# One product group of the first superstep split in two, under a newly drawn order of all instructions (linear attention and gated MLP, one core)

## The chip, the cores and the metric

The kernel runs on one core of a Trainium2 chip. The metric is the device time of one execution in microseconds; the engines are named PE (TensorE, matrix products), DVE (VectorE), ACT (ScalarE), POOL (GpSimd) and SP (SyncE, which here issues all DMAs).

## The reference

Two stages. The first is a recurrence over 768 positions for 4 x 8 heads of width 40, the second a gated MLP over the 3072 tokens that come out of it:

```python
for t in range(S):
    y[:, :, t] = einsum('bhd,bhde->bhe', rt, state)
    Sa = einsum('bhde,bhe->bhd', state, at)
    state = state * wt[:, :, None, :] - einsum('bhd,bhe->bhde', Sa, bt) + einsum('bhd,bhe->bhde', vt, kt)
...
h = x @ w_in                                     # 3072x320 @ 320x2048
g = h * erf(softplus(h))
out = g @ w_out                                  # 2048x320
```

All arrays are float32 values; the MLP's weights arrive in a wider type and are rounded to float32 on the chip.

## The kernel before

**Stages.** The 768 positions are cut into 6 stretches of 128 for each of 2 groups of 16 heads: 12 *supersteps* (0 to 11), each of 4 *chunks* of 32 positions. Superstep 0 delivers the first 256 rows of x; superstep q's MLP part can start when its four chunks are done. The state is carried from chunk to chunk (tile MT), so the chunks are a chain. The MLP is not: it is 96 blocks of 512 values per partition (8 to a superstep) that only need x.

**Names.** Below, "op q.c" is the operation of chunk c in superstep q; letters a to d tell the copies of one chunk apart.
- Once a superstep: w (load), wchk, scanS and scanP (L439, L443, two scans each), rG: the running products of the decays.
- A, ahead of the chain, per chunk: kba (load), ab and bk (DVE L472, L477), A (PE L482), Am a/b (DVE L489), bT and bTc (PE L500 and a copy), zs (DMA, waits for ab), AD (DMA of the masked products to DRAM).
- T, per superstep, for all four chunks at once: Ti and Ap (DMAs back from DRAM, after the last AD), 14 pairs Tm/Ts (DVE L529, L530: a triangular inverse), TD and tb (DMAs out and back), R (DVE L538), W, Wm, DAD (PE L547 and a copy), Tb (DVE L554).
- Chain, per chunk: zmm a/b (two copies of MT), Z (PE L593), zt (copy), U (PE L602), us (copy), zu a to d (four copies into tile Vu, L612), and beside these pmt and ysM (PE L618 and a copy of the old state), UT (PE L627), vtu (copy), PQ (PE L636), PQm (DVE L639, into Vu), then **MY** (PE L647 and L651), MT (DVE L654, state += MY's first 40 columns), Ym (DVE L658, the rows of y from the other 32 columns). MTs scales the state between supersteps.
- Out and in: xw (DMA of y to DRAM), xr (DMA back as x), xh and xl (x rounded and the rest), mm1 (PE L823), hc, tanh, ln, ln2, exp, nd, rho, gelu, E, G (ACT and DVE), mm2 (PE L878).
- Weights, once, at the start: wd (loads of 512 KB; "wd" of w_in, "wdo" of w_out), w1, w3, w5 (DVE L737 to L739), whi, whr, wr0 (ACT), wd_ (PE L754, L755), wlo (copies).
- warm (PE L422): 190 products whose result nobody reads, all ahead of the third mm1.

**MY.** For each of 4 pairs j, four products `sg x Vu` of 72 columns write the bank `my`: columns 0 to 39 are the state's update and need zu and the v rows of Vu, columns 40 to 71 are the rows of y and need PQm. Four products `sm x rt` of 32 columns are then added to columns 40 to 71.

**Order.** Nothing is scheduled on the chip: `Plan.schedule` returns the list ORDER, a permutation of the 4630 operations, and ENGINES, one letter for each (which of its allowed engines runs it). Each engine works through its own operations strictly in the list's order and waits at the head of its queue; data dependences (and reuse of buffers) are the waits. So an operation late in the list holds back what stands behind it on its engine, also DMAs on SP.

Of the kernel before, what the change touches and what calls it, by code (L numbers as in the profile page):

```python
# [1008 lines left out]
```

## Time and profile before

| | |
|---|---|
| runs shown | 756.65, 761.78, 762.60 us; median 761.78 |
| profiled execution | span 754.8 us, first to last instruction; its own device time is not listed apart from these runs |
| PE | 722.7 us busy (96%), 190 warm products included |
| DVE, ACT, POOL | 643.1 (85%), 573.3 (76%), 5.6 (1%) |
| DMA | 94.63 MB, all issued by SP |
| mean granted TensorE clock | 0.991 of full speed |

The profile is one execution. Its 40 slices of 18.9 us show PE at 9 tenths or more from slice 11 on, and at 6 to 9 before. PE's busy share of the opening says little by itself, as most of what runs there until about 110 us are weight preparation and warm products. The timeline of an engine tells what stood at the head of its queue, and in brackets how long it idled before and for whom.

### The profile page before, as it was taken

The page shows a single profiled execution, that of the slowest core. Times are in us where ns is not written, and L with a number is a line of the kernel's source. Part 1 is how long each engine was busy: PE and PEld are TensorE (multiplying, and loading weights), DVE is VectorE, ACT ScalarE, POOL GpSimd, SP SyncE. Part 2 cuts the span into 40 slices and gives each one's busy share as a digit, 9 for nine tenths or more (in the row PEclk, how much of TensorE's full clock was granted, in tenths as well). Part 3 has the DMA queues.
Part 4 walks back from the last instruction along what each step waited for, and adds up shares of the span by engine and source line. Part 5 has one row for each costly group of instructions (what it writes and reads, how often), then busy time and mean ns, then how long its engine had stood idle before and what let it go on. Part 6 is the DMA issues. An engine that isn't in the chain of part 4 may idle for free.

```text
span 754.8 us, 32087 instructions
## 1 busy us (share of the span) xinstructions
PE 722.7 (96%) x13807; PEld 570.4 (76%) x13807; DVE 643.1 (85%) x1461; ACT 573.3 (76%) x1122; POOL 5.6 (1%) x15
## 2 busy tenths in 40 slices
...
GB/s 255 175 256 197 142 160 153 144 124 122 129 147 121 131 140 126 118 125 126 131 126 136 132 134 139 130 104 138 140 103 115 124 112 92 104 41 61 21 17 22
DMA packets 165616, 94.63 MB, mean 125 GB/s; under 512 B 115452, under 2 KB 148988, under 8 KB 165468
## 3 DMA queue, kind: packets, MB, share of 16 engines
...
q8 instruction: 110, 1.80, 1.1%
...
HBM read 73.48 MB, written 14.16 MB: 116 GB/s over the span
## 4 chain that ended last, share of the span: by engine, by line
PE 83%; ACT 5%; DVE 5%; DMA 3%; issue 2%; SPq 1%; DVEq 0%
PE po L878 29%; PE ph L823 22%; PE my L647 4%; PE ph L422 4%; PE pA L547 4%; PE pQ L636 4%; PE pA L482 3%; PE my L602 2%; PE my L593 2%; PE pA L500 2%; PE pQ L618 2%; PE my L651 2%; SPq L381 1%; PE pQ L627 1%; ACT l L831 1%
## 5 line engine op out<-in xcount | busy, mean ns | idle before, releaser
L878 PE MATMUL po<-wo,h 128*128 128x320 f32 x768 | 265.2, 454 | 1.1 <-DVE h L869 1.1
L878 PEld LDWEIGHTS po<-wo,h 128*128 128x128 f32 x768 | 125.5, 189 | 30.5 <-DVE h L869 1.9
L831 ACT ACTIVATE l<-l 128x512 f32<-128x512 f32 x192 | 111.0, 624 | 8.3 <-DVE nd L856 7.5
L823 PE MATMUL ph<-xh,wih 128*128 128x256 f32 x384 | 113.8, 378 | 0.0
L823 PEld LDWEIGHTS ph<-xh,wih 128*128 128x128 f32 x384 | 69.5, 190 | 24.1 <-issue 0.3
L823 PE MATMUL ph<-xh,wil 128*128 128x256 f32 x384 | 77.2, 282 | 0.7 <-issue 0.7
L823 PE MATMUL ph<-xl,wih 128*128 128x256 f32 x384 | 76.9, 282 | 0.0
L856 DVE TENSOR_TENSOR nd<-l,r 128x512 f32<-128x512 f32 x96 | 64.3, 687 | 9.6 <-ACT r L831 8.4
L868 DVE TENSOR_TENSOR l<-l,r 128x512 f32<-128x512 f32 x96 | 64.5, 682 | 1.2 <-ACT l L831 0.4
L869 DVE SCALAR_TENSOR_TENSOR h<-l,h 128x512 f32<-128x512 f32 x96 | 64.6, 684 | 0.5
L857 DVE SCALAR_TENSOR_TENSOR r<-nd,r 128x512 f32<-128x512 f32 x96 | 64.2, 683 | 0.2
L831 ACT ACTIVATE l<-h 128x512 f32<-128x512 f32 x96 | 57.6, 627 | 4.2 <-DVE h L377 3.1
L823 PEld LDWEIGHTS ph<-xh,wil 128*128 128x128 f32 x384 | 59.5, 190 | 0.7 <-issue 0.7
L375 ACT COPY h<-ph 128x512 f32<-128x512 f32 x84 | 48.9, 583 | 14.2 <-PE ph L823 13.4
L823 PEld LDWEIGHTS ph<-xl,wih 128*128 128x128 f32 x384 | 59.2, 189 | 0.0
L831 ACT ACTIVATE r<-r 128x512 f32<-128x512 f32 x96 | 55.3, 623 | 0.4
L831 ACT ACTIVATE r<-l 128x512 f32<-128x512 f32 x96 | 54.9, 621 | 0.3
L422 PE MATMUL ph<-d 104*128 104x512 bf16 x190 | 53.3, 401 | 1.6 <-DVE d L392 1.6
L823 PE MATMUL ph<-xl,wir 128*128 128x256 f32 x192 | 54.2, 282 | 0.0
L823 PE MATMUL ph<-xh,wir 128*128 128x256 f32 x192 | 54.1, 282 | 0.0
L375 ACT COPY Zm<-MT 40x320 f32<-40x320 f32 x62 | 28.3, 457 | 28.7 <-DVE MT L654 24.1
L489 DVE TENSOR_TENSOR Zs<-pA,tri 64x256 f32<-64x256 f32 x96 | 40.6, 423 | 11.1 <-PE pA L482 6.0
...
## 6 DMA issues: line engine op xcount, KB each, us to landing
...
```

The lines of the kernel that those rows point to most:

```text
L375: self.nc.scalar.copy(o, i)
L422: P.add("warm", "PE", lambda e: nc.tensor.matmul(s.ph[1], s.d1[:, :128], s.d1[:, :512], start=True, stop=True), ["d1"], ["phw"], -1e3, 0.22)
L489: P.add("Am", "DVE", lambda e, x=x, xs=xs: nc.vector.tensor_tensor(out=zx[64:128, x], in0=pz[xs], in1=s.tri[xs, None, :].to_broadcast([64, ...
L547: nc.tensor.matmul(pw[js, i, ts], l[js, i], r[js, i, ts], start=True, stop=True)
L636: nc.tensor.matmul(pq[i % 2 * 64:i % 2 * 64 + 64, i // 4, i // 2 % 2], vr[:, 256 + n_ * 64:320 + n_ * 64], vr.rearrange("p (a x) -> p a x" ...
L823: nc.tensor.matmul(ph[:, j * 256:j * 256 + 256], a[:k, fs], b[:k], start=(m == 0), stop=(m == 7))
L831: self.P.add(name, "ACT", lambda e: nc.scalar.activation(out=o, in_=i, **kw), rd, wr + ["act"], pr, 0.62)
L856: P.add("nd", [("DVE", 0.69)], lambda e, r=r, l=l, nd=nd: s.eng(e).tensor_tensor(out=nd, in0=l, in1=r, op=ALU.mult), [("l", il), ("r", ir) ...
L857: P.add("rho", "DVE", lambda e, r=r, nd=nd: nc.vector.scalar_tensor_tensor(out=r, in0=nd, scalar=2 * C4, in1=r, op0=ALU.add, op1=ALU.mult) ...
L868: P.add("E", [("DVE", 0.69)], lambda e: s.eng(e).tensor_tensor(out=l, in0=l, in1=r, op=ALU.mult), [("r", ir)], [("l", il)], pr)
L869: P.add("G", "DVE", lambda e: nc.vector.scalar_tensor_tensor(out=h, in0=l, scalar=-1.0, in1=h, op0=ALU.add, op1=ALU.mult), [("l", il)], [( ...
L878: nc.tensor.matmul(po, h[:, bs], s.wo[:, f], start=(f == 0), stop=(f == 15))
```

## The change

Two things. (1) In superstep 0 alone (`NSPLIT = 1`, q < 1), MY is issued as two operations: MYs, the `sg x Vu` products on columns 0 to 39, which no longer waits for PQm, sm and rt; and MYy, the same products on columns 40 to 71 and the `sm x rt` products. MT waits for MYs alone, Ym for MYy alone. From superstep 1 on MY is one operation as before.

```diff
+NSPLIT = 1
...
-            ms("zmy", s.my[:, x], 0.0, ["my", "pz"], (("DVE", 0.6),))
+            ms("zmy", s.my[:, x], 0.0, ["my", "myr", "pz"], (("DVE", 0.6),))
...
+        py = my[:, :, :, 40:72].rearrange("p x j t -> p j x t")
+        split = q < NSPLIT
+
+        def mmy(e, state, rows):
+            fs = slice(0 if state else 40, 72 if rows else 40)
             for j in range(NP // 2):
                 for h in range(2):
                     for x in range(2):
                         xs = slice(x * 64, x * 64 + 64)
-                        nc.tensor.matmul(my[h * 64:h * 64 + 40, x, j], sg[xs, j, h], vu[xs, j // 2 * 2 + h, j % 2], start=True, stop=False)
-                for h in range(2):
+                        nc.tensor.matmul(my[h * 64:h * 64 + 40, x, j, fs], sg[xs, j, h], vu[xs, j // 2 * 2 + h, j % 2, fs], start=True, stop=not rows)
+                for h in range(2 * rows):
...
+        if split:
+            P.add("MYs", "PE", lambda e: mmy(e, True, False), [("sg", ig)] + kst, ["my"], pr, 0.6)
+            P.add("MT", "DVE", fmt, ["my"], ["MT"], pr, 0.49)
+            P.add("MYy", "PE", lambda e: mmy(e, False, True), [("sg", ig)] + krow, ["myr"], pr, 0.8)
+        else:
+            P.add("MY", "PE", lambda e: mmy(e, True, True), [("sg", ig)] + kst + krow, ["my", "myr"], pr, 0.95)
+            P.add("MT", "DVE", fmt, ["my"], ["MT"], pr, 0.49)
...
-        P.add("Ym", ..., ["my"], [("p", ip, c)], pro, 0.42)
+        P.add("Ym", ..., ["myr"], [("p", ip, c)], pro, 0.42)
```

(2) ORDER and ENGINES are other lists altogether (4634 operations). The DMAs' places in SP's queue, loads of input blocks and weights included, differ too. 271 operations run on another engine, most of them copies (108 of the 192 zu, 31 of the 96 zmm). The stretches of both lists that the prediction speaks of, with the numbers replaced by names ("warm*3" are three in a row):

```
PE, old list: 86 warm ahead of A 0.0
PE, new list: 56 warm ahead of A 0.0, with wd_ 0[0] and pmt 0.0 among them;
  A 0.0 | warm*4 | wd_ 0[1] | warm*6 | bT 0.0 | warm*2 | wd_ 0[2] | warm*13 | A 0.1

PE, old list, superstep 0's chain (74 warm):
U 0.0 | warm*2 | UT 0.0 | warm*3 | PQ 0.0 | A 1.1 | warm*1 | MY 0.0 | bT 1.1 | pmt 0.1 | warm*1 | Z 0.1 | warm*2 |
U 0.1 | warm*1 | A 1.2 | warm*1 | UT 0.1 | warm*3 | bT 1.2 | warm*1 | PQ 0.1 | warm*3 | A 1.3 | warm*1 | MY 0.1 |
bT 1.3 | warm*4 | pmt 0.2 | warm*1 | Z 0.2 | warm*1 | U 0.2 | UT 0.2 | warm*5 | PQ 0.2 | warm*6 | MY 0.2 | warm*1 |
wd_ 0[19] | warm*2 | wd_ 0[18] | pmt 0.3 | warm*1 | Z 0.3 | warm*1 | U 0.3 | warm*3 | UT 0.3 | warm*4 | PQ 0.3 |
warm*3 | MY 0.3 | warm*10 | Z 1.0 | ... | A 2.0 | warm*1 | U 1.0 | bT 2.0 | UT 1.0 | mm1 0[0]
PE, new list (71 warm):
U 0.0 | warm*3 | UT 0.0 | warm*1 | MYs 0.0 | warm*2 | A 1.1 | warm*1 | PQ 0.0 | Z 0.1 | warm*1 | bT 1.1 | MYy 0.0 |
pmt 0.1 | warm*1 | U 0.1 | warm*1 | A 1.2 | warm*2 | MYs 0.1 | UT 0.1 | warm*1 | bT 1.2 | warm*4 | PQ 0.1 | A 1.3 |
Z 0.2 | MYy 0.1 | warm*2 | pmt 0.2 | bT 1.3 | U 0.2 | warm*8 | MYs 0.2 | warm*1 | UT 0.2 | warm*5 | PQ 0.2 | warm*5 |
wd_ 0[19] | warm*1 | Z 0.3 | pmt 0.3 | MYy 0.2 | warm*3 | U 0.3 | warm*1 | UT 0.3 | warm*3 | wd_ 0[18] | PQ 0.3 |
MYs 0.3 | warm*3 | MYy 0.3 | pmt 1.0 | warm*7 | Z 1.0 | warm*3 | W 1 | warm*1 | DAD 1.0 | warm*6 | DAD 1.1-3 | warm*2 |
A 2.0 | warm*1 | U 1.0 | warm*2 | bT 2.0 | UT 1.0 | mm1 0[0]

DVE, old: Am 0.3 | w3 0[6] | w5 0[6] | scanS 1 | rG 1 | wlo 0[10] | scanP 1 | Tm 0 ... (one wlo among the 14 pairs)
DVE, new: Am 0.3 | w5 0[4] | w1 0[6] | w1 0[7] | w3 0[7] | w5 0[7] | w3 0[6] | scanS 1 | w1o[1] | w5 0[6] | rG 1 |
  scanP 1 | Tm 0 ... (w1 0[8] after the 4th pair, w3 0[8] ahead of the last Ts)
DVE, new, chain: Am 1.0 | ab 1.1 | us 0.0 | zu 0.0c | zu 0.0b | w5o[4] | MT 0.0 | zmm 0.1 | Am 1.1 | PQm 0.0 | bk 1.2 |
  ab 1.2 | us 0.1 | zu 0.1a | zu 0.1d | Am 1.2 | MT 0.1 | bk 1.3 | ab 1.3 | Ym 0.0 | PQm 0.1 | Am 1.3 | scanS 2 | w1o[5] |
  Ym 0.1 | rG 2 | scanP 2 | MT 0.2 | zmm 0.3 | 4 pairs Tm/Ts 1 | PQm 0.2 | 10 pairs | zu 0.3b | vtu 0.3 | Ym 0.2 | PQm 0.3 |
  MT 0.3 | MTs 1 | Ym 0.3 | w3o[5] | wlo | R 1 | bk 2.1 | w1o[8] | bk 2.0 | w1o[6] | w5o[5] | ab 2.0 | w3o[8] | w3o[6] |
  wlo | w5o[8] | xl 0[1] | Tb 1 | ysM 1.0 | Am 2.0 | xl 0[0] | xl 0[2]   (old: MT 0.2 among the pairs, vtu 0.3 on ACT)
ACT, new: ... | zu 0.0a | zu 0.0d | bTc 1.0 | vtu 0.0 | ... | zt 1.0 | xh 0[1] | xh 0[0] | xh 0[2] | us 1.0

SP, old: Ti 0 | rv | zs 0.2 | wd 0[9] | wdo[0] | wd 0[8] | Ap 0 | ... ; xw 0 (4) | rt | rv | zs 2.0b | xr 0 (4)
SP, new: Ti 0 | Ap 0 | wd 0[8] | kba 1.0 | wdo[2] | wdo[0] | ... ; tb 1 | xw 0 (4) | zv 1.1 | wdo[9] |
  xr 0[1] | xr 0[2] | xr 0[3] | zs 2.0a | xr 0[0]

PE, superstep 1, old: PQ 1.2 | mm1 | MY 1.2 ... U 1.3 | UT 1.3
PE, superstep 1, new: PQ 1.2 | mm1 | mm1 | MY 1.2 ... U 1.3 | mm2 | UT 1.3
```

## Rows read from the trace of the kernel before

**Rows 1.** Windows: us, then busy time of each engine, granted clock, DMA share, GB/s
```profile
116.00:200.00 84.00, 77.52 (x1721) 65.41 (x1720) 74.14 (x183) 68.08 (x139) 0.00 (x0) 1.00 0.56 133
200.00:700.00 500.00, 496.39 (x10211) 406.50 (x10211) 439.75 (x1010) 424.93 (x822) 0.00 (x0) 1.00 0.51 120
```

**Rows 2.** Timeline of PE, opening: start, us, line, out<-in, [idle before <-releaser]
```profile
1.62 21.34 PE L422 MATMUL ph<-d 104*128 104x512 bf16 x85 [1.62 <-DVE d L392]
...
23.97 0.69 PE L482 MATMUL pA<-Ab,bk 104*64 104x64 f32 x16
```

**Rows 3.** Timeline of DVE around the first triangular inverse
```profile
37.03 0.69 DVE L738 SCALAR_TENSOR_TENSOR r<-wo,r 128x512 int32<-128x512 int32 x1
...
38.37 2.35 DVE L439 TENSOR_TENSOR_SCAN Wt<-Pr,d 104x516 f32<-104x516 f32 x2
...
43.63 0.17 DVE L529 TENSOR_TENSOR tmp<-Ti 128x14 f32<-128x14 f32 x1
...
50.21 0.19 DVE L530 TENSOR_TENSOR Ti<-Ti,tmp 128x14 f32<-128x14 f32 x1
...
51.56 0.43 DVE L737 TENSOR_SCALAR r<-wo 128x512 int32<-128x512 int32 x1 [0.50 <-DMA wo<-in_moe_w_in]
```

**Rows 4.** Timeline of PE, superstep 0's four chunks
```profile
69.86 0.42 PE L602 MATMUL my<-zt,Tb 32*32 32x40 f32 x24
...
73.82 0.34 PE L647 MATMUL my<-Vu,sg 64*40 64x72 f32 x8
73.97 0.25 PE L651 MATMUL my<-Rt,Sm 40*40 40x32 f32 x8
74.04 0.32 PE L647 MATMUL my<-Vu,sg 64*40 64x72 f32 x8
...
76.69 0.49 PE L593 MATMUL my<-Zm,Zs 96*32 96x40 f32 x32 [0.47 <-ACT Zm L375]
...
80.78 0.73 PE L636 MATMUL pQ<-vt 104*64 104x64 f32 x16
...
86.17 0.49 PE L593 MATMUL my<-Zm,Zs 96*32 96x40 f32 x32
...
96.56 0.49 PE L593 MATMUL my<-Zm,Zs 96*32 96x40 f32 x32
```

**Rows 5.** Groups by line, 69 to 112 us: busy us, mean ns, idle before
```profile
L422 PE MATMUL ph<-d 104*128 104x512 bf16 x71 | 20.3, 382 | 0.0
```

**Rows 6.** Timeline of DVE around the second triangular inverse
```profile
90.56 0.17 DVE L529 TENSOR_TENSOR tmp<-Ti 128x14 f32<-128x14 f32 x1 [0.28 <-DMA Ti<-AD]
...
93.62 0.49 DVE L654 TENSOR_TENSOR MT<-MT,my 104x320 f32<-104x320 f32 x1 [0.84 <-PE my L651]
...
106.61 0.71 DVE L538 STREAM_TRANSPOSE T<-Tb 128x512 f32<-128x512 f32 x1 [0.71 <-DMA Tb<-TD]
```

**Rows 7.** Timeline of SP: DMA issues
```profile
42.76 0.43 SPq L381 DMA_DIRECT2D wo<-in_moe_w_in  x1
...
98.61 1.17 SPq L381 DMA_DIRECT2D TD<-Ti  x2
...
104.20 1.59 SPq L381 DMA_DIRECT2D xd<-Pr  x4
...
107.87 3.14 SPq L381 DMA_DIRECT2D xr<-xd  x4
```

**Rows 8.** Timeline of ACT and of PE at the MLP's start
```profile
112.74 0.41 ACT L375 CAST xh<-xr 128x256 fp32r<-128x256 f32 x1 [0.22 <-DMA xr<-xd]
...
115.83 0.48 PE L823 MATMUL ph<-xh,wih 128*128 128x256 f32 x2
```

**Rows 9.** Waits of PE from 116 to 200 us: total, times, longest
```profile
PE my L647 <- DVE tmp L529: 1.0, 1, 1.0
```

**Rows 10.** Windows around PE's long idle stretch (columns as in rows 1)
```profile
46.00:48.00 2.00, 0.00 (x0) 0.00 (x0) 1.80 (x9) 0.00 (x0) 0.00 (x0) 1.00 0.99 389
...
60.00:62.00 2.00, 2.00 (x8) 1.08 (x7) 1.05 (x2) 0.00 (x0) 0.00 (x0) 0.51 0.72 211
```

More of the change, by code (lines that the diff above doesn't have):

```diff
@@ L165 @@
-SSSSVVVPVPVAASAPVPAPVPVVSSSSSSVAPAPASSAVPVPVPVPVVSSSSSSVVPVPVVVVVPVPVPVPVVSSSSSSVAPVPAAASAPVPAPVPVVSSSSVPVVSVVSVVSSVVAAAAAAAAAAAAAAVVVVVVVVAAAAAPPVAPPAAPPVAVVPPPPPPVAVVPPPPVVPPPPVV
-PPPPVSVSAAAAAAAAAAAAAAVVVVVVVVAAAAAPPVAPPVAPPVAVVPPPPPPAAVVPPPPVVPPPPVVPPPPAAAAAAAAAAAAAAVVVVVVVVAAAAAVVPPPPVVPPPPVVPPPPVVPPPPASAS
+SSVVGVGGAGGGGGGGAAAAGVVGAAAPPPPPPPPPPPPPPPPPPPPPPPPPPPPPPPPPPPPPPPPPPPPPPPPPPPPPPPPPPPPPPPPPPPPPPPPPPPPPPPPPPPPPPPPPPPPPPPPPPPPPPPPPPPPPPPPPPPPPPPPPPP
+PPPPPPPPPPPPPPPPPPPPPPPPPPPPPPPPPPPPPPPPPPPPPPPPPPPPPPPPPPPPPPPPPPPSAVVAVSVSSVPVVSSPASVSSVPVVSSPASVSSVPVVSSPVSVSSVPVVSSPASSSSAAVVVVVVVVVVVVVVVVVVVVVVV
@@ new lines @@
+VVVVVSSSSVPPPPAPPPPVSVVVAPAPASVVVAPAPVSVVVAPVPASVVVAPAPASVVVAPAPASVVVAPAPASVVVAPVPVSVVVAPAPVSVVVAAAPVAPAASVVVAAAPVVPAASVVVSVVVSVVVSVVVSVVVSVVVSVVVSVVV
+SVVVSVVVSAVVAVSVSSVPVVSSPASVSSVPVVSSPASVSSVPVVSSPASVSSVPVVSSPASSSSSSAAPVPVAVVAPAPAPVPVPVSSSSSSVVPAPVVAAVPAPAPVPVPVSSSSSSAAPAPAAAAAPAPAPVPVPVSSSSSSVVPA
+PAAVAAPAPVPVPVPVSSSSSSSSAAVVVVVVVVVVVVVVVVVVVVVVVVVVVVSSSSVPPPPAPPPPVSAVSAVSSAVPPAAPPVAPPAAPPVAAAAAAAAAAAAAAAVVVVVVVVAAAAAPPAAPPAAPPAAVVPPPPPPAAVVPPPP
+VVPPPPVVPPPPSAVVVVSVSSVPVVSSPASVSSVPVVSSPASVSSVPVVSSPASVSSVPVVSSPASSSSSSVAAPAPASAVAPVPVPVPVVSSSSSSAAPAPAVSASPVPAPVPVVSSSSSSVVPAPASASAPAPAPVPVVSSSSSSAV
@@ new lines @@
+PAPASVAVPAPVPVPVVSSSSSSSSAAVVVVVVVVVVVVVVVVVVVVVVVVVVVVSSSSVPPPPVPPPPVSAVSAVSSAVAAAAAAAAAAAAAAVVVVVVVVAAAAAPPAAPPAAPPAAVVPPPPPPAAVVPPPPVVPPPPVVPPPPASV
+SAAAAAAAAAAAAAAVVVVVVVVAAAAAPPAAPPAAPPAAVVPPPPPPAAVVPPPPVVPPPPVVPPPPSAVVAVSVSSVPVVSSPASVSSVPVVSSPASVSSVPVVSSPASVSSVPVVSSPASSSSSSVVAPVPASASVPAPAPVPVVSS
+SSSSAVPAPASAAAPAPAPVPVVSSSSSSVVPAPAVASSPAPAPVPVVSSSSSSVAPAPAVAVVPAPAPVPVVSSSSSSSSAAVVVVVVVVVVVVVVVVVVVVVVVVVVVVSSSSVPPPPVPPPPVSVVSAVSSVVAAAAAAAAAAAAAA
+VVVVVVVVAAAAAPPAAPPAAPPAAVVPPPPPPAAVVPPPPVVPPPPVVPPPPASASAAAAAAAAAAAAAAVVVVVVVVAAAAAPPAAPPAAPPAAVVPPPPPPAAVVPPPPVVPPPPVVPPPPSAVVVVSVSSVPVVSSPASVSSVPVV
@@ new lines @@
+SSPASVSSVPVVSSPASVSSVPVVSSPASSSSSSVAAPAPAVAVVPAPAPVPVVSSSSSSVAPAPAAAAAPAPAPVPVVSSSSSSAAPAPAASSAPAPVPVPVVSSSSSSAVPAPVAAVVPAPAPVPVVSSSSSSSSAAVVVVVVVVVVV
+VVVVVVVVVVVVVVVVVSSSSVPPPPAPPPPVSVVSVVSSVVAAAAAAAAAAAAAAVVVVVVVVAAAAAPPAAPPAAPPAAVVPPPPPPAAVVPPPPVVPPPPVVPPPPASASAAAAAAAAAAAAAAVVVVVVVVAAAAAPPAAPPAAPP
+AAVVPPPPPPAAVVPPPPVVPPPPVVPPPPSAVVVVSVSSVPVVSSPVSVSSVPVVSSPASVSSVPVVSSPASVSSVPVVSSPVSSSSSSVVAPVPAVVAVPVPAPVPVVSSSSSSVAPAPASAVAPAPAPVPVVSSSSSSAAPAPASSV
+APAPAPVPVVSSSSSSAVPAPVAVSSPAPVPVPVVSSSSSSSSAAVVVVVVVVVVVVVVVVVVVVVVVVVVVVSSSSVPPPPVPPPPVSAVSAVSSVVAAAAAAAAAAAAAAVVVVVVVVAAAAAPPAAPPAAPPAAVVPPPPPPAAVVP
@@ new lines @@
+PPPVVPPPPVVPPPPASASAAAAAAAAAAAAAAVVVVVVVVAAAAAPPVAPPAAPPAAVVPPPPPPAAVVPPPPVVPPPPVVPPPPSAVVVVSVSSVPVVSSPASVSSVPVVSSPASVSSVPVVSSPASVSSVPVVSSPVSSSSSSVVVP
+APASVVVPVPAPVPVVSSSSSSVAPAPASAAAPAPAPVPVVSSSSSSVAPAPASAVAPAPVPVPVVSSSSSSVAPVPAVAAVPAPAPVPVVSSSSSSSSAAVVVVVVVVVVVVVVVVVVVVVVVVVVVVSSSSVPPPPAPPPPVSAVSVV
+SSVVAAAAAAAAAAAAAAVVVVVVVVAAAAAPPAAPPAAPPAAVVPPPPPPAAVVPPPPVVPPPPVVPPPPASVSAAAAAAAAAAAAAAVVVVVVVVAAAAAPPAAPPAAPPAAVVPPPPPPVAVVPPPPVVPPPPVVPPPPSAVVVVSV
+SSVPVVSSPASVSSVPVVSSPASVSSVPVVSSPASVSSVPVVSSPASSSSSSVAAPAPVSASVPVPAPVPVVSSSSSSAVPAPASSAAPAPAPVPVVSSSSSSAAPAPASVSAPAPAPVPVVSSSSSSVAPAPAVAVVPAPAPVPVVSSS
```

46 lines of the change are left out of this document (17 added, 29 removed), and 271 rows, old and new, of the table ORDER.

## The prediction

> **What bounds the kernel now.** I read the windows first. From 200 to 700 us PE is busy 496.4 of 500 us, and from 116 to 200 us 77.5 of 84 [rows 1]: once the MLP's products run, PE is the bound, and 84.00 - 77.52 + 500.00 - 496.39 = 10.1 us is all the idleness there is to win behind that point. So the time is the start of mm1, 115.83 us [rows 8], plus PE's fixed work, plus at most those 10.1 us. Then I read the timelines of the first 116 us, engine by engine, because there PE's busy share hides that it runs warm products: 71 of them, 20.3 us, from 69 to 112 us [rows 5]. There the bound is a chain of latencies: the first triangular inverse at 43.6 to 50.4 us [rows 3], its round trip through DRAM, U 0.0 at 69.86 and the chunks' Z at 76.69, 86.17 and 96.56, some 10 us apart [rows 4]; beside it the second inverse, 90.56 until TD at 98.61 and R at 106.61 [rows 6, 7]; and x out and back, xw at 104.20, xr from 107.87 [rows 7]. The chunks and the second inverse meet at mm1.
>
> **Part 1, the opening.** The old list holds PE with 86 warm products ahead of A 0.0, 21.34/85 = 0.25 us each, so that it starts at 23.97 [rows 2]. The new one has 56, one wd_ and pmt: 1.6 + 56 x 0.25 + 1.3, about 17. That is 7 us earlier, but A 0.1 stands behind 25 more warm products, two wd_ and bT, 8 us, at 25.2; walking DVE's queue on from there at 0.4 to 0.7 us an operation, with its waits for A 0.2 and A 0.3, I get Am 0.3 done at 33.5 against 37.0 [rows 3]. What follows is DVE's queue. Old: from 37.03 to 43.63, 6.6 us, until the first Tm. New: eight weight conversions more or less in the same place, five at 0.69 less 0.03 of overlap, three at 0.43, two scans at 2.35 and rG, 9.5 us: 43.0. The inverse itself took 6.8 us with one wlo of 0.3 in it; now it holds w1 and w3 of load 8, 1.1 us: it ends at 50.5 against 50.4. So **the 3.5 us won ahead of it are spent on DVE, and this part is worth 0**. Bounds: -0.6 (no extra in the loop counts), and +2.8: in the old list load 8 was issued at 42.76 and its w1 waited for it until 51.56, 8.8 us [rows 3, 7]; in the new list it is issued behind Ti and Ap, which I put at 38.9, and 8.8 later is 47.7, while its w1 is due at 44.9. I take 0, as it then has fewer loads ahead of it. U 0.0 stays at 69.9, since bT 1.0 still stands ahead of it in both lists.
>
> **Part 2, the split.** What it takes away: MT waits for zu, no longer for UT, vtu, PQ, PQm. What it adds: 16 products a chunk, as MYs + MYy are 48 against 32. The rows price a group of four at 0.15 us (72 columns, 73.82 to 73.97) and 0.07 (32 columns, to 74.04) [rows 4]; four groups a chunk of 40 columns cost between 0.3 and 0.6 us more, I take 0.4, in the place of warm products, which hide it, 20.3 us of them [rows 5]; without that cover it would be 1.6 us over four chunks. The Trainium skill, "TensorEngine Tiling (Array Packing)", section "Instruction Overhead", speaks against splitting columns: a product of 1 column takes as long as one of 60, about 60 cycles, so cutting 72 columns in 40 and 32 would cost nearly the whole group again. By it the extra, estimated at 0.15 us a group, is 0.6 us a chunk; if it lay on the path in all four the sum below would be 2.4 us higher, 762.2 in place of 759.8. The row of 0.07 us for 32 columns speaks against the rule.
>
> Chunk by chunk, with PE in order: *Chunk 0*: zu are done at 71.6, MYs runs to 72.2, MT (DVE, behind one conversion) to 72.9, zmm to 73.5; but Z 0.1 stands behind A 1.1 and PQ 0.0, 0.7 us each, and PQ behind vtu: 74.3 against 76.69, -2.4. *Chunk 1*: U 0.1 now stands behind MYy 0.0, which waits for PQm: 76.9, only -0.7. MYs 0.1 78.7, MT to 79.9, zmm on ACT behind whr and vtu to 81.0; Z 0.2 behind bT, four warm, PQ and A 1.3: 82.6 against 86.17, -3.5. *Chunk 2*: U 0.2 85.2, MYs done 88.0; MT 0.2 stands behind the two scans of superstep 2, which end at 89.5; zmm to 90.6, Z 0.3 behind UT, PQ, ten warm and wd_: 92.6 against 96.56, -4.0. *Chunk 3*: U 0.3 95.1; its vtu and one zu now run on DVE, behind the 28 steps of the second inverse. Queued behind that wait are PQ 0.3, MYs 0.3, MT, MTs and Ym.
>
> **Part 3, what is late next.** The second inverse needs Am 1.3, AD, Ti: A 1.3 moves by 0.4 us only, and DVE is free at 90.6. So Tm 1 starts at 90.4 against 90.56. It no longer has MT 0.2 in its midst (0.49 and a wait of 0.84 [rows 6]): it ends at 97.1 against 98.5, TD goes at 97.2 (98.61), and with the old 8.0 us to R, R is at 105.2 (106.61). MT 0.3 is done at 99.6, Ym 0.3 at 101.1, xw at 101.7 against 104.20, three xr from 105.3 on. But **the fourth xr stands behind zs 2.0a on SP**, which waits for ab 2.0, seven operations behind R on DVE, 109.3: so it goes at 110.2, and its x lands at 112.7, where xh waited before too, 112.74 [rows 8]. DVE has ten operations of 0.4 to 0.7 us between R and Tb 1 (111.7), then ysM and Am 2.0, xl until 114.5, and PE UT 1.0: mm1 at 114.8 against 115.83. **The chunks' 4.0 us arrive as -1.0.**
>
> **Part 4, behind the start.** The new list puts a second mm1 between PQ 1.2 and MY 1.2, where PE waited 1.0 us for PQm [rows 9]: -1.0. The other waits there keep their neighbours, and the units' lists are the old ones in the main. For the rest of the 10.1 us I see neither gain nor loss; bounds -5 and +5, half of them, as each wait depends on a neighbour that was drawn anew.
>
> **Sum:** 0 + 0 - 1.0 - 1.0 = -2.0 us. Against the profiled execution: its span is 754.8, so 752.8. That span is 7.0 below the median of the runs shown, which carry the launch's ends and scatter by 6 us (756.65 to 762.60); on the median it is 761.78 - 2.0 = **759.8 us**. 1% of the median, 7.6 us, is about what a measurement of this kernel can tell from no change: faster is below 754.2, slower above 769.4.
>
> **Rivals.**
> *A, all of the split arrives:* x and the second inverse follow Z 0.3, -4.0, and part 4's 1.0: 756.8. For it: xw moves by 2.5. Against: the inverse starts when Ti lands, the fourth xr waits for R. Chance 0.13.
> *B, faster by more than 1%:* A, and the new order fills half of the 10.1 us: 761.78 - 4.0 - 5.0 = 752.8. For it: short waits of that kind are what an order can change. Against: the fill of the MLP's pipeline has the same blocks and units in both lists. Chance 0.2.
> *C, the split's effect is void:* MT done early, and all else as late as before, because the second inverse and x decide alone: 761.8, and load 8 in the first inverse makes it 764.6. Chance 0.13.
> *D, slower:* PE's clock. When PE stood idle (0.00 of 2 us at 46 to 48) its granted clock fell to half, and it was 0.51 still at 60 to 62 [rows 10], that is 1.2 GHz; during the chunks warm products kept it at full. The new list has its longest empty place there: PQ 0.3 waits for vtu behind the second inverse on DVE. If Ti lands 3 us later than before (93.6 instead of 90.56), U 0.3 to PQ 0.3 leaves PE idle for about 4 us, as then; and the 13 us of PE work from PQ 0.3 to mm1 (25 warm, 5.5 us, and 7.7 of products) run at half the clock. With 10 us of it at half rate: 3.0 + 5.1 = 8.1, 769.9. It decides from a start of the inverse at about 93; for it: the three warm and a wd_ there cover only 1.5 us; against: nothing that I see moves Ti that far. Chance, with other delays of over 1%, 0.12.
>
> **How the numbers follow.** My forecast 0.42, A 0.13, B 0.2, C 0.13, D 0.12. Faster is B, 0.20; slower is D, 0.12; the rest is within 1%, 0.68. The range runs from B with a little scatter, 751.5, to just below D, 768.5, which takes in the +2.8 of part 1 and the +5 of part 4 (767.6); some 0.1 is left out on either side.
>
> **What would show it.** Right: the first Tm within 1 us of 43.6; Z 0.1 to 0.3 earlier by 2 to 4 us; the second inverse's start within 1 us of 90.6 and R 1 to 2 us earlier; vtu 0.3 on DVE behind the last Ts; one xr issued after zs; mm1 at 114 to 115.5. Wrong: the first inverse over before 48 (then part 1 is a gain and all behind it moves), mm1 before 112, a granted clock below 1 from 97 to 110, or PE idle from 116 to 700 us by more than 13 or less than 7 us.

## The result, and the profile after

The changed kernel took **771.11 us** (median of 11 runs, 763.8 to 781.82); the kernel before took 761.78 beside it (11 runs, 756.65 to 767.39). The ratio is 1.011 with a 95% interval of 1.0066 to 1.0155: slower by 8.4 us (5 to 12), outside the forecast range of 751.5 to 768.5. The profiled execution took 770.99 us, span 768.8, mean granted clock 0.976 (before: 0.991). Medians here count every run; ratios, here and below, leave disturbed runs out, so that the two can differ by some us.

Windows of the changed kernel, columns as in [rows 1]:

```profile
116.00:200.00 84.00, 78.67 (x1604) 64.82 (x1603) 70.47 (x156) 61.39 (x126) 0.00 (x0) 0.91 0.52 124
200.00:700.00 500.00, 491.64 (x10245) 401.89 (x10244) 442.09 (x1047) 411.79 (x790) 0.00 (x0) 1.00 0.50 119
```

Where the forecast expected 10.1 us of idleness, as before, there are 5.3 + 8.4 = 13.7, and from 116 to 200 us the granted clock is 0.91 instead of 1.00. The timeline of PE through the start (compare [rows 2, 4, 8]):

```profile
18.01 0.69 PE L513 MATMUL pA<-Ab,bk 104*64 104x64 f32 x16
...
69.67 0.51 PE L633 MATMUL my<-zt,Tb 32*32 32x40 f32 x32
...
74.14 0.49 PE L624 MATMUL my<-Zm,Zs 96*32 96x40 f32 x32
...
84.29 0.69 PE L513 MATMUL pA<-Ab,bk 104*64 104x64 f32 x16 [1.95 <-DVE Ab L503]
84.91 0.49 PE L624 MATMUL my<-Zm,Zs 96*32 96x40 f32 x32
...
109.06 1.34 PE L578 MATMUL pA<-T,Ap 32*32 32x16 f32 x128 [1.68 <-DVE T L569]
...
120.56 0.48 PE L864 MATMUL ph<-xh,wih 128*128 128x256 f32 x2
```

Lines are 31 to 41 higher than before. A 0.0, U 0.0 and Z 0.1 come within 1.0 us of the forecast (17, 69.9, 74.3). Then A 1.3 waits 1.95 us, Z 0.2 is 2.3 us behind its forecast, W 1 waits 1.68 us for R, and mm1 starts at 120.56: forecast 114.8, before 115.83. DVE shows what A 1.3 waited for (compare [rows 3, 6]):

```profile
44.26 0.17 DVE L560 TENSOR_TENSOR tmp<-Ti 128x14 f32<-128x14 f32 x1
...
51.32 0.17 DVE L561 TENSOR_TENSOR Ti<-Ti,tmp 128x14 f32<-128x14 f32 x1
...
82.44 0.69 DVE L508 TENSOR_TENSOR bk<-bk,Wt 104x512 f32<-104x512 f32 x1 [2.00 <-DMA bk<-in_kba_e]
...
93.97 0.17 DVE L560 TENSOR_TENSOR tmp<-Ti 128x14 f32<-128x14 f32 x1
...
108.30 0.71 DVE L569 STREAM_TRANSPOSE T<-Tb 128x512 f32<-128x512 f32 x1 [2.56 <-DMA Tb<-TD]
```

The first inverse runs from 44.26 to 51.5 (forecast 43.0 to 50.5). bk 1.3 waits 2.00 us for its block load, and the second inverse starts at 93.97, not at 90.4. SP's issues (compare [rows 7]): that load, kba 1.3, at 76.67; then TD, xw, three xr, and the fourth behind zs 2.0a, which is where the forecast had put it:

```profile
76.67 1.46 SPq L412 DMA_DIRECT2D bk<-in_kba_e  x1
...
100.81 1.16 SPq L412 DMA_DIRECT2D TD<-Ti  x2
...
106.25 1.82 SPq L412 DMA_DIRECT2D xd<-Pr  x4
...
110.44 1.70 SPq L412 DMA_DIRECT2D xr<-xd  x3
112.19 0.87 SPq L412 DMA_DIRECT2D Zs<-Ab  x1
113.10 0.48 SPq L412 DMA_DIRECT2D xr<-xd  x1
```

Windows around the wait ahead of W 1 (compare [rows 10]):

```profile
106.00:108.00 2.00, 1.38 (x36) 0.58 (x35) 0.00 (x0) 0.00 (x0) 0.00 (x0) 1.00 0.60 110
110.00:112.00 2.00, 2.00 (x73) 1.19 (x62) 2.00 (x5) 1.03 (x3) 0.00 (x0) 0.52 0.89 264
116.00:118.00 2.00, 2.00 (x19) 1.04 (x17) 0.81 (x3) 0.09 (x1) 0.00 (x0) 0.50 0.38 104
```

PE idled from 107.4 to 109.1; from 110.1 to 120.3 its granted clock is 0.50, 1.2 GHz. From W 1 to mm1 PE ran without a pause and took 11.50 us, against 8.45 in the trace of before, whose clock was full there. In all, the changed kernel's trace has 34 us at 1.2 GHz between 48 and 750 us, the first trace of before 10.

PE's waits from 116 to 200 us (compare [rows 9], whose wait of MY is gone, as forecast):

```profile
PE my L633 <- ACT zt L406: 1.7, 2, 1.2
PE my L624 <- issue: 1.5, 1, 1.5
PE pQ L649 <- DVE MT L689: 1.1, 1, 1.1
```

The wait that is gone was not for PQm, as the prediction read [rows 9]:

```profile
142.83 0.39 PE L647 MATMUL my<-Vu,sg 64*40 64x72 f32 x5 [1.03 <-DVE tmp L529]
```

In the trace of before PQm 1.2 was done at 141.48, ahead of the wait, which began at 141.80. MY 1.2 went on 0.13 us behind the landing (142.70) of a copy zu that SP issued as a DMA; in `before_again` and `h_new_start` below, it starts 0.14 us behind the landing of the same copy.

The cover of the extra products was there: 68 warm products between 69 and 116 us (compare [rows 5]; their mean is longer for the time at 1.2 GHz):

```profile
L453 PE MATMUL ph<-d 104*128 104x512 bf16 x68 | 21.4, 420 | 0.0
```

### The profile page after: what moved, and what is told of

The parts are those of the page before. It is cut to its first block, busy times and chain, and to the rows that moved or that the text cites. A ratio compares the mean times of both kernels' runs of the same rounds, so it can differ in the third digit from the quotient of the medians.

```text
span 768.8 us, 32350 instructions
## 1 busy us (share of the span) xinstructions
PE 732.4 (95%) x13935; PEld 575.8 (75%) x13935; DVE 653.6 (85%) x1494; ACT 561.3 (73%) x1084; POOL 5.7 (1%) x16
## 3 DMA queue, kind: packets, MB, share of 16 engines
q8 instruction: 112, 1.84, 1.0%
## 4 chain that ended last, share of the span: by engine, by line
PE 75%; DVE 10%; DMA 6%; issue 3%; ACT 2%; SPq 2%; DVEq 0%; ACTq 0%
PE po L919 25%; PE ph L864 22%; PE pA L578 4%; PE my L681 4%; PE pQ L667 3%; PE pA L513 3%; PE ph L453 3%; PE pA L531 2%; PE pQ L649 2%; PE my L624 2%; PE my L633 2%; SPq L412 2%; PE my L685 2%; DMA Tb<-TD 2%; DMA TD<-Ti 1%
## 5 line engine op out<-in xcount | busy, mean ns | idle before, releaser
L919 PE MATMUL po<-wo,h 128*128 128x320 f32 x768 | 248.6, 447 | 1.3 <-DVE ob L408 0.6
L919 PEld LDWEIGHTS po<-wo,h 128*128 128x128 f32 x768 | 131.8, 190 | 38.6 <-DVE h L910 1.8
L872 ACT ACTIVATE l<-l 128x512 f32<-128x512 f32 x192 | 112.6, 625 | 8.1 <-DVE nd L897 7.1
L864 PE MATMUL ph<-xh,wih 128*128 128x256 f32 x384 | 102.8, 349 | 0.0
L864 PEld LDWEIGHTS ph<-xh,wih 128*128 128x128 f32 x384 | 64.5, 191 | 14.6 <-ACT h L406 0.3
L406 ACT COPY h<-ph 128x512 f32<-128x512 f32 x78 | 45.0, 582 | 18.3 <-PE ph L864 18.2
L453 PE MATMUL ph<-d 104*128 104x512 bf16 x190 | 55.9, 419 | 1.6 <-DVE d L423 1.6
L681 PE MATMUL my<-Vu,sg 64*40 64x72 f32 (+2 forms) x1664 | 47.2, 226 | 2.5 <-ACT zt L406 0.7
```

The source lines that it names most:

```text
L406: self.nc.scalar.copy(o, i)
L453: P.add("warm", "PE", lambda e: nc.tensor.matmul(s.ph[1], s.d1[:, :128], s.d1[:, :512], start=True, stop=True), ["d1"], ["phw"], -1e3, 0.22)
L681: nc.tensor.matmul(my[h * 64:h * 64 + 40, x, j, fs], sg[xs, j, h], vu[xs, j // 2 * 2 + h, j % 2, fs], start=True, stop=not rows)
L864: nc.tensor.matmul(ph[:, j * 256:j * 256 + 256], a[:k, fs], b[:k], start=(m == 0), stop=(m == 7))
L872: self.P.add(name, "ACT", lambda e: nc.scalar.activation(out=o, in_=i, **kw), rd, wr + ["act"], pr, 0.62)
L919: nc.tensor.matmul(po, h[:, bs], s.wo[:, f], start=(f == 0), stop=(f == 15))
```

## The experiments

Theories as they were formed: **1**, idle stretches of 1.3 to 2 us bring PE's clock down, and that is the loss. **2**, the late block load behind chunk 3's A starts it. **3**, the split's own products. **4**, the loss is in the start, up to mm1. **5**, it is in the new order behind mm1. **6**, PE's instructions arrive late in packets.

### Clock and split (theories 1 to 3)

`e_new_fill`: new list; PE's queue alone is edited.

```
+ 8 warm ahead of A 1.3;  + 8 warm ahead of W 1
  ... A 1.3 | mm1 0[8] | MY 1.1 | mm1 0[10] | mm1 0[9] | pmt 1.2 | Z 1.2 | mm1 0[11] | U 1.2 ... Z 2.0 | mm2 0[8] | W 2
```

> The new list and the split, with PE's holes filled: 8 warm products more ahead of A 1.3 and 8 ahead of W 1, and three pieces of PE's old order put back in superstep 1 (mm1 0[10] and 0[9] behind MY 1.1, mm1 0[11] ahead of U 1.2, Z 2.0 and one mm2 ahead of W 2). DVE, ACT and SP are as in the new list. Theory 1 (PE's idle stretches of 1.3 to 2 us bring the granted clock down to half): the falls at 86, 110, 144 and 168 us are gone, 34 us at half become about 14, of which about half is time: 761 us (757 to 765). Theory 2 (the late block load behind chunk 3's A starts it, and the clock only follows): A 1.3 is as late as in the new list, mm1 starts at about 119, 768 or more. Theory 3 (the split's own products and MYy ahead of U cost it): 770, as the new list.

774.61 us, ratio 1.0126 (1.0037 to 1.0215). Theory 1 missed by 13.6 us. The falls at 86, 110, 144 and 168 us were gone, but behind DAD 1.0 PE now stood still for 2.25 us, marked "issue" (it waited for nothing), the clock fell there, and mm1 came at 123.94.

`e_old_cold`: kernel before, `warm` 115 to 188 with 8 columns.

```diff
+            w = 8 if 115 <= i <= 188 else 512
-  ... nc.tensor.matmul(s.ph[1], s.d1[:, :128], s.d1[:, :512], ...
+  ... nc.tensor.matmul(s.ph[1][:, :w], s.d1[:, :128], s.d1[:, :w], ...
```

> The old list and no split; the 74 warm products from U 0.0 to the first mm1 have 8 columns instead of 512, so that PE stands idle in their place. Theory 1: the granted clock is at half for most of 70 to 116 us, the chunks' PE work (some 4 us a chunk) takes up to twice as long, mm1 starts 6 to 14 us later, 768 to 776 us. Theories 2 and 3: warm products are nothing but filling, the block loads come as before and nothing is split: 760 to 764, or up to 3 us less as they stand in nobody's way.

766.64 us, ratio 1.0046 (1.0006 to 1.0086). From 62 us to mm1 the clock was at 1.2 GHz for 38 us, and mm1 still came at 119.83; the kernel lost 3.5 us (0.5 to 6.6), not the 6 to 14 that theory 1 had forecast. Where the start is a chain of latencies, a low clock costs little. The edit also takes the warm products' own work away, so it does not price a low clock where PE itself is on the path, from W 1 to mm1. That stretch took 9.44 us here, at 1.2 GHz with short warm products. With the full ones at 1.2 GHz it took 11.50 us in the changed kernel and 11.58 in `e_old_pad128` below, which has the old list, both without a pause of PE; at 2.4 GHz it took 8.45 in the trace of before. So theory 1 falls for the chunks; from W 1 to mm1 the low clock goes with 3 us.

`e_old_split` and `e_old_split_warm`: the old list with the split, ordered by hand.

```
chunks 0 to 2 on PE: ... MYs c | PQ c | ... | Z c+1 | MYy c ...   DVE: MT c ahead of PQm c   ACT: zu c | vtu c | zmm c+1
e_old_split_warm: the same, + 16 warm ahead of W 1
```

> The old list with the split alone: MYs of chunks 0 to 2 ahead of PQ, MT ahead of PQm, the copies of MT right behind, the next Z ahead of MYy; chunk 3 has MYs and MYy side by side. The number of warm products is the old one, 74. Theory 1: Z 0.3 comes 4 to 6 us earlier, but the second inverse and so W 1 do not, so PE runs out of warm products and stands idle for about 4 us more ahead of W 1; the clock falls there: 764 to 770 us. Theory 3 (split itself costs): Z 0.3 comes less than 2 us earlier or later, and 766 or more whatever the clock. If neither, and the split is harmless or a gain: 758 to 762.

> The same as the old list with the split alone, and 16 warm products more ahead of W 1 (0.22 us each, 3.5 us), which cover the time that the earlier chunks leave empty. Theory 1: granted clock at full from 62 to 750 us as in the kernel before, 757 to 762 us. Theory 3: 766 or more. Forecast on record for the split (the chunks' gain arrives as 1 us): 760.

765.30 us, ratio 1.0044 (0.9999 to 1.0089), and 772.51, ratio 1.016 (1.007 to 1.0249). The first is inconclusive on the split: my order left PE idle for 4.08 us ahead of Z 0.3, and mm1 came at 120.28. In the second the 16 products overshot: R was done at 113.2, W 1 came at 116.33, mm1 at 127.72. Warm products are no free filling where PE is next on the path.

`e_new_nosplit`: the new list with `NSPLIT = 0`.

```diff
-NSPLIT = 1
+NSPLIT = 0
  # MY in MYy's place; MY 0.2 directly behind its five warm products, MT 0.2 after the 5th Tm 1
```

> The new list without the split: MY of superstep 0 is one operation again, in MYy's place; MT, its copies and the next Z are moved behind it as far as they need, all else is the new list. If the split itself cost the 9 us: 762 to 765. If the new order does (theories 5 and 6): chunks 1 to 3 come 2 to 4 us later, the second inverse and so mm1 about the same, and the stretches behind mm1 stay: 768 to 775.

776.77 us, ratio 1.0195 (1.0143 to 1.0248): 0.85% above the changed kernel's ratio, mm1 at 124.71. The split is not the loss; in this list it is worth some 6 us by the ratios, though the intervals overlap. Theory 3 falls.

### Start or rest (theories 4 and 5)

```
h_new_start: new list, new engines and the split up to and with mm1 0[0] (711 operations); all else as in the old list
h_old_start: old list without the split up to mm1 0[0]; all else as in the new list
before_again: the kernel before, a second trace
```

> A list put together from both: the new list with the split up to and with mm1 0[0] (711 operations, on the new engines), and behind it all other operations in the old list's order on the old engines. Theory 4 (the cost is in the start: the second inverse late behind the block load of A 1.3, and the clock between W 1 and mm1): mm1 0[0] at 119 to 121 us and the old 633 to 636 us behind it, 766 to 769. Theory 5 (the cost is in the order behind the start, waits of PE in superstep 1 and stretches without instructions at W): the start's share is at most 2 us, 762 to 765.

> The reverse, without the split (MY as one operation everywhere): the old list up to and with mm1 0[0], and all else in the new list's order on the new engines. Theory 5: mm1 0[0] at 115 to 119 and some 640 us behind it, with PE's waits ahead of pmt 1.2 and U 1.2 and the stretches marked issue at the W of later supersteps: 767 to 770. Theory 4: 761 to 765, as before.

> The kernel before once more, for a second trace. The profiled execution of before was its fastest of three (756.65), with the granted clock at half for 15 us; its other runs have 20 to 40 us at half by their mean clock. Expected: 760 to 766 us, the same waits and the same places of the stretches marked issue, but more falls of the clock behind mm1, 2 to 4 us of which are time. If the first trace was typical: the same start (116) and no fall between 62 and 750.

767.97 us, ratio 1.0046 (1.0005 to 1.0087); 776.37, ratio 1.0108 (1.0008 to 1.0208); 764.96. The new rest alone costs 8.3 us (0.6 to 15.9), as much as the whole change, the new start alone 3.5 (0.4 to 6.7). So neither theory holds alone: 767.97 is what theory 4 had forecast for the new start (766 to 769), and 776.37 is above what theory 5 had for the new rest (767 to 770). The swap hardly moves the places of theory 6 below: mm1 is PE's instruction no. 3556 with the new start and 3293 with the old, 263 apart, so that either rest is moved by 7 against a multiple of 256. PE's timeline in `before_again`:

```profile
86.07 0.69 PE L482 MATMUL pA<-Ab,bk 104*64 104x64 f32 x16 [1.03 <-ACT Wt L447]
...
119.09 0.48 PE L823 MATMUL ph<-xh,wih 128*128 128x256 f32 x2
```

and in `h_new_start`:

```profile
82.82 0.49 PE L624 MATMUL my<-Zm,Zs 96*32 96x40 f32 x32
...
92.55 0.49 PE L624 MATMUL my<-Zm,Zs 96*32 96x40 f32 x32
...
107.98 1.26 PE L578 MATMUL pA<-T,Ap 32*32 32x16 f32 x128 [1.37 <-DVE T L569]
...
119.56 0.56 PE L864 MATMUL ph<-xh,wih 128*128 128x256 f32 x1
```

The same old list has A 1.3 at 82.34 in its first trace and at 86.07 here, mm1 at 115.83 [rows 8] and 119.09; the same new start has A 1.3 at 84.29 in the changed kernel and at 82.20 in `h_new_start`. So the late load of the changed kernel's trace (theory 2) is scatter between executions, and so is its later R (108.30 and 107.22 with the new start, 106.61 and 110.17 with the old), 1.7 of the 4.7 us at its mm1. The other 3 us are not: W 1 to mm1 took 11.50 and 11.58 us in the two traces of the new start, both at 1.2 GHz for some 10 us, and 8.45 and 8.15 in the two of before, both at 2.4. W 1 in the first trace of before, in the chain that ended last:

```profile
107.38 0.44 PE pA L547 x32
```

The first trace of before was a lucky one: it is its 756.65, 5 us below its median.

Behind mm1 the traces part. PE's waits from 200 to 700 us, the kernel before, then the changed kernel, then `h_old_start`:

```profile
PE pA L547 <- issue: 1.7, 2, 1.3
PE ph L823 <- issue: 0.7, 2, 0.5
```

```profile
PE pA L578 <- issue: 4.0, 3, 2.0
PE pA L578 <- DVE T L569: 1.7, 2, 1.5
```

```profile
PE pA L578 <- issue: 3.6, 3, 1.3
PE pA L578 <- DVE T L569: 2.3, 2, 1.7
PE po L919 <- issue: 1.8, 1, 1.8
PE my L681 <- DMA Vu<-in_v_x: 1.6, 1, 1.6
```

In the changed kernel the largest are those of the tiny products of W and DAD (L578), for DVE's R and for "issue". In all PE idles for 3.6 us of this stretch in the first trace of before and 6.8 in `before_again`, 8.4 in the changed kernel and 13.3 in `h_old_start`.

### Packets of instructions (theory 6)

In the changed kernel's timeline of PE two such stretches look like this:

```profile
165.53 0.26 PE L624 MATMUL my<-Zm,Zs 96*32 96x40 f32 x2
167.24 0.49 PE L624 MATMUL my<-Zm,Zs 96*32 96x40 f32 x30 [1.46 <-issue]
...
607.91 1.23 PE L578 MATMUL pA<-Tb,W 32*32 32x16 f32 x125
611.11 0.23 PE L578 MATMUL pA<-Tb,W 32*32 32x16 f32 x3 [1.97 <-issue]
```

PE stops in the middle of an operation, 2 products into Z, 125 into DAD, where nothing is waited for. The table of DMA queues has the instructions' own queue:

```profile
q8 instruction: 112, 1.84, 1.0%
```

112 packets of 16 KB, for 28,114 instructions of PE (products, weight loads, semaphore events): 256 in a packet with little left over. Counted from 0, PE's instructions at these two places are no. 5313 and 23745, and those at the other stretches of this kind no. 7874, 10178, 14785 and 19138: each is 193 or 194 past a multiple of 256, and so they are in the trace of before (5313, 7617, 18881) and, behind mm1, in all 20 traces, but for one stretch of 0.34 us in `e_old_split_warm`. At 165.78 the packet had started at 164.82 and landed, and PE went on 1.46 us later. From the place before, 256 instructions back, there had been 1.4 us of work, and 2.1 us ahead of the stop at 609, as W and DAD are 256 instructions in 1.26 us each. Short work makes a stop likely and not certain: behind 128 us, in all 20 traces, PE stopped for over 0.25 us at 75 of the 120 places that it reached within 3 us of the place before, and at 6 of the 1305 that it reached after 5 us or more, as among mm1 and mm2. The Trainium skill, "Runtime: NRT & Kernel Launch", section "Instruction fetch mechanics", has the blocks of 256 instructions and calls the crossing of one "mostly hidden"; the trace agrees with the blocks, and with "mostly" by their number (7 stops at some 110 crossings in the changed kernel); where tiny products are packed the crossing is not hidden: the stops are of 0.3 to 3.75 us.

Five experiments move these places without touching the order.

```diff
+            w = [512] + [8] * N if i == 3 else [8] if 3 < i <= 3 + M else [512]
-            P.add("warm", "PE", lambda e: nc.tensor.matmul(s.ph[1], ..., s.d1[:, :512], ...
+            P.add("warm", "PE", lambda e, w=w: [nc.tensor.matmul(s.ph[1][:, :c], ..., s.d1[:, :c], ...) for c in w][-1], ...
  # e_old_pad N=52, M=12; e_new_pad 13, 3; e_old_pad40 20, 5; e_old_pad128 and e_new_pad128 64, 15
```

> The old list, with 52 products of 8 columns more among the first warm products, and 12 warm products cut from 512 to 8 columns so that A 0.0 comes no later. Nothing else changes but the number of instructions ahead of everything on PE, by 104. Theory 6: PE's idle stretches marked issue stand at every 256th instruction of PE (counted from the 193rd or 194th), where a packet of 16 KB on the instruction queue lands late, because the 256 before it took less than 4 us, as the 128 products of W do. Then 104 instructions move all these places; worked out from the times of the trace of before with 4 us for a packet, the sum of such stretches rises by 8 to 10 us at most, and I expect 4 to 8 us and a fall of the clock behind the longest: 767 to 774. Without theory 6: no change, 761 to 765.

> The new list and the split, with 13 products of 8 columns more among the first warm products and 3 warm products cut to 8 columns: 26 instructions more ahead of everything on PE. Theory 6: worked out from the trace of after, this is the best place for the packets, 4 us less of idle stretches marked issue than without (those at 165.8, 223.4, 325.0, 495.6 and 609.1 us shrink or go), and fewer falls of the clock: 763 to 768. Theories 4 and 5 without theory 6: 769 to 773, as after.

> The old list with 20 products of 8 columns more among the first warm products and 5 warm products cut to 8 columns: 40 instructions more ahead of everything on PE. Theory 6: worked out from the times of before, this is the best place for the packets of instructions, 3 us less of idle stretches than without any, 760 to 764 against 764 to 765. If the kernel with 104 more was slower for another reason than the place of the packets (its products themselves, a later A 0.0): 764 to 770.

> The old list with the same 64 products (128 instructions). If the old list as it stands lies at one of few good places: 772 to 782, as with 40 and 104 instructions (774.6 and 781.6). If the two slow places were chance: 762 to 768.

> The new list and the split, with 64 products of 8 columns more among the first warm products (and 15 warm products cut to 8 columns): 128 instructions more ahead of everything on PE, half a packet. If the new list is slow only because of where its packets fall (theory 6 alone): a place half a packet away may well be as good as the old list's, 762 to 768. If its order behind mm1 is worse at any place (theory 5 and 6): 770 to 778, as at the two places seen (771 and 776).

| instructions moved | old list: us, ratio (95%) | new list: us, ratio (95%) |
|---|---|---|
| 0 | 761.8 to 766.2, 1 | 771.11, 1.011 (1.0066 to 1.0155) |
| 26 | | 776.29, 1.0136 (1.005 to 1.0222) |
| 40 | 774.56, 1.015 (1.0095 to 1.0204) | |
| 104 | 781.56, 1.0216 (1.0153 to 1.0279) | |
| 128 | 784.02, 1.0259 (1.0201 to 1.0317) | 786.77, 1.0333 (1.0292 to 1.0373) |

The places matter: 20 to 64 tiny products before 20 us, and the same old order is 11 to 20 us slower. In the new list 128 instructions cost 17 us more, and 26 make no clear difference (the intervals overlap). Most of the loss is behind the start: from mm1 to the end `e_old_pad128` took 653 us, against 633 and 638 in the two traces of the kernel before; its mm1 came at 123.69, against 115.83 and 119.09. In `e_old_pad128`, PE's timeline:

```profile
449.08 1.37 PE L548 MATMUL pA<-Tb,W 32*32 32x16 f32 x126
453.02 0.20 PE L548 MATMUL pA<-Tb,W 32*32 32x16 f32 x2 [2.57 <-issue]
...
506.90 0.48 PE L603 MATMUL my<-zt,Tb 32*32 32x40 f32 x29
509.84 0.34 PE L603 MATMUL my<-zt,Tb 32*32 32x40 f32 x3 [2.47 <-issue]
```

Again at 193 or 194 (no. 16833 and 19138), and the clock fell to 1.2 GHz at each. The forecasts for 104 and 128 instructions were all too low (at most 774, 782 and 778), and my forecast of good places failed twice: 26 and 40 instructions were worked out with 4 us for every packet, where the packets themselves took 0.9 to 2.3 us, and neither won anything. The size of one stretch, which varies with the packet's own delay, is not settled.

### A version with the split (all with the old rest)

```
h_new_start_w: h_new_start, five of the six warm between DAD 1.0 and DAD 1.1 moved ahead of W 1
h_w_m16: that, 8 warm less ahead of A 0.0;   h_w_p16: that, 8 products of 8 columns more there
h_drop8: h_new_start without the five warm behind DAD 1 and three ahead of DAD 1.1
h_w_drop8: h_new_start_w without the five warm behind DAD 1 and three ahead of W 1
```

> The list of new start and old rest, with five of the six warm products between DAD 1.0 and DAD 1.1 moved ahead of W 1; the number of instructions stays. Theory 1, cut down to this one place (PE runs out of warm products for 1.4 to 1.7 us ahead of W 1, the clock is at half from 110 to 120 us and costs 3 us from W 1 to mm1): no fall at 110, W 1 to mm1 in 8.5 to 9.5 us instead of 11.5, 3 us less than without, 764 to 766. Otherwise: 767 to 769, as without.

> New start, five warm products moved ahead of W 1, old rest, as before, but with 8 warm products less ahead of A 0.0 (182 in all, 16 instructions less). The start is as without, mm1 at 116 to 118. Behind it, only the packets fall 16 instructions later: 760 to 766 if that takes the waits at 168 and 276 us away, 768 to 774 if it brings others.

> The same list with 8 products of 8 columns more among the first warm products (two cut to 8 columns), 16 instructions more: packets fall 16 instructions earlier. 760 to 766 if the place is better, 768 to 776 if worse; either way mm1 at 116 to 119 and the difference behind it, as stretches marked issue and falls of the clock.

> New start with the split, old rest; 8 warm products are left out between DAD 1.0 and mm1 0[0] (the five behind DAD 1 and three of the six ahead of it), where PE's own work is on the way to mm1. Ahead of that place the packets fall as in the list without the change (1.3 us marked issue), behind it 16 instructions later as in the list with 8 products less at the beginning (1.7 us marked issue behind mm1 in its trace, against 4 to 6). Theory 6: mm1 about 1.8 us earlier, 117 to 119, 634 to 636 behind it, 760 to 763, which beats both kernels. If the packets' place can't be set like this: 765 to 768.

> The same with five warm products moved from between DAD 1.0 and DAD 1.1 to ahead of W 1; the 8 left out are the five behind DAD 1 and three of the eight ahead of W 1. Theory 1 at this place and theory 6: mm1 at 115.5 to 118, 634 to 636 behind it, 758 to 762. Otherwise 764 to 768.

Ratios: 1.0038 (0.9999 to 1.0077), 1.0026 (1.0001 to 1.0051), 1.0031 (0.9992 to 1.007), 0.9971 (0.9934 to 1.0008) and 1.0004 (0.9967 to 1.0042); medians 767.97, 765.07, 767.93, 766.2 and 767.1. All lie below the changed kernel's 1.011, the first and the third with intervals that overlap with its own; none is clearly faster than the one before, and the forecasts of 760 to 763 and 758 to 762 for the last two were missed. `h_new_start_w` did not win the 3 us at W 1: the hole was filled, a packet stopped DAD 1 for 1.84 us at 109.6, and the clock fell from 112.8 to 119.7.

## Why the prediction was wrong

**Where the loss is.** In the 15 traces without the five of theory 6, the time from mm1 to PE's end is one constant and three terms: PE's idleness at packets (marked issue, at 193 or 194 of 256), its other waits, and half of the time at 1.2 GHz (the same products of one mm1 took 1.87 us at 147 us, at 1.2 GHz, and 1.04 at 132 us, at 2.4).

| from mm1 to the end, us | packets | other waits | clock | rest | sum |
|---|---|---|---|---|---|
| old rest, mean of 11 traces (632.8 to 641.6) | 4.1 | 7.5 | 4.2 | 620.8 | 636.7 |
| new rest, mean of 4 traces (642.0 to 652.0) | 6.9 | 10.3 | 7.1 | 620.8 | 645.1 |
| the changed kernel's trace | 6.4 | 8.3 | 6.8 | 620.6 | 642.0 |

The rest is 619.7 to 622.3 in all 15, so the three terms hold nearly all of what differs. The two groups stand 8.4 us apart: 2.8 for packets, 2.8 for waits, 2.9 for the clock. They do not overlap, but only by 0.4 us (641.6 and 642.0), and three of the four new rests carry other edits too, so 8.4 is not the changed kernel's own figure. Its own trace is 5.3 us above the mean of the old rest: 2.3 for packets, 0.8 for waits, 2.6 for the clock. The other 3 us of the measured 8.4 are ahead of mm1: W 1 to mm1 took 11.50 us, against 8.45 and 8.15.

**Point by point.** *Part 1* held: the inverse ran from 44.26 to 51.5 (forecast 43.0 to 50.5, "within 1 us of 43.6"). *Part 2* held where A 1.3 was not late: `h_new_start` has Z 0.2 at 82.82 and Z 0.3 at 92.55, forecast 82.6 and 92.6. The extra products cost no more than was taken (MYs, then the first and the last rows of MYy):

```profile
102.18 0.52 PE L681 MATMUL my<-Vu,sg 64*40 64x40 f32 x32
...
103.38 0.28 PE L681 MATMUL my<-Vu,sg 64*40 64x32 f32 x8
103.48 0.26 PE L685 MATMUL my<-Rt,Sm 40*40 40x32 f32 x8
...
103.94 0.26 PE L685 MATMUL my<-Rt,Sm 40*40 40x32 f32 x8
```

The last row of MY 0.0 in the trace of before, which began at 73.82 [rows 4]:

```profile
74.59 0.25 PE L651 MATMUL my<-Rt,Sm 40*40 40x32 f32 x8
```

MYs takes 0.5 us, MYy 0.8, MY took 1.0: 0.3 more, where 0.4 was taken. A group of 32 columns took 0.10 us and one of 72 took 0.15 [rows 4]; the rule of the Trainium skill, "TensorEngine Tiling (Array Packing)", section "Instruction Overhead", by which the 32 columns would have cost nearly as much as the 72, does not show in these rows. *Part 3* held in its bookkeeping (the fourth xr behind zs 2.0a at 113.10, xh last) but not in its times: the second inverse started at 93.97 and, with A 1.3 on time, at 92.51 in `h_new_start`, where Ti landed 5.1 us behind its issue at 87.43, against 3.7 in the trace of before. R came at 107.22 and 108.30, forecast 105.2, which is within the scatter of the old start (106.61 and 110.17). From R to mm1 the forecast had 9.6 us, with DVE's queue (Tb 1, xl) on the path; it took 12.3 in both traces, against 9.2 and 8.9 before, and in the changed kernel's trace PE itself was on the path, without a pause from W 1 on, most of it at 1.2 GHz. So mm1 came at 119.56 and 120.56, against 115.83 and 119.09 of before: +2.6 between the means, where -1.0 was forecast.

**Two steps failed.** The larger is *part 4*: "the units' lists are the old ones in the main. For the rest of the 10.1 us I see neither gain nor loss; bounds -5 and +5". The wait of MY 1.2 went (-1.0), for another reason than the one read into [rows 9], but the stretch behind mm1 lost 5.3 us in the changed kernel's own trace, and 8.4 in the mean of the four new rests. The ten microseconds were read as idleness to be won, not as the result of places that fit: the same 4630 operations with their packets 128 instructions further on lose 20 us. And a bound on idleness alone left out that low clock goes with the stops and waits, at half a us for each at 1.2 GHz behind mm1. The other is the end of *part 3*, "The chunks' 4.0 us arrive as -1.0": the term from R to mm1 was 9.6 us on DVE's queue and measured 12.3, on PE at 1.2 GHz, with 12 warm products among its work. Of the signs of being wrong, PE's idleness of more than 13 us came true (13.7); the clock fell at 110.1, just behind the stretch that was to be watched.

**Rival D** named the sign, the clock and nearly the time (769.9), and was right in part. Its condition came (the second inverse at 93.97), and so did 10 us at 1.2 GHz ahead of mm1. But PE idled ahead of W 1 and not ahead of PQ 0.3, as U 0.3 came at 98.62, 3.5 us behind its forecast too; the low clock cost 3 us there, not 5.1; and D had nothing behind mm1, where more than half of the loss is. So the nearness of its 769.9 is in good part luck. It had 0.12 because I took the first trace's full clock from 62 to 750 us for the kernel's habit. `before_again` had 15 us at half there.

**Still open:** how much of the loss behind mm1 is the new order itself, and how much the places of its packets. At a displacement of 128 both lists are slow, 1.0259 and 1.0333, 0.7% apart; a place that suits the new list as 0 suits the old was not found in two tries. How far a list must move to lose is not mapped either: the old rest lies 33 instructions further on in `e_old_split_warm`, and took 636.2 us there, no more than the mean. And no run shows W 1 to mm1 of the new start at the full clock without a stop, so its 3 us are put down to the clock by comparison, not by a test.
